# Eight PSUM tiles of one bank each in place of one tile of four banks and four of one

## The chip, the cores and the metric

The kernel runs on one core of a Trainium2 chip. The metric is the device time of one execution in microseconds (us), the median of three. The core has five engines with a queue each: TensorE (PE: matmuls and transposes, results in PSUM), VectorE (DVE), ScalarE (ACT), GpSimd (POOL) and SyncE (SP, which issues the DMAs here). PSUM has eight banks of 512 fp32 columns per partition. Instructions of one queue run in order.

## The reference

Two blocks. The first is a linear attention whose features are products of two sketches; the second takes its output as tokens and runs causal softmax attention in four experts, of which each token uses the best two.

```python
def phi(x):                                   # q, k: (4, 4, 1088, 32), 8 x 8 = 64 features
    a = np.einsum('rd,bhsd->bhsr', S1, x)
    b = np.einsum('rd,bhsd->bhsr', S2, x)
    return np.einsum('bhsi,bhsj->bhsij', a, b).reshape(*x.shape[:-1], r * r)
q_p, k_p = phi(q), phi(k)
kv = np.einsum('bhsf,bhsd->bhfd', k_p, v)
z = np.sum(k_p, axis=2)
x = einsum(q_p, kv) / (einsum(q_p, z) + 1e-6)   # then (4, 1088, 128)

logits = x @ w_gate                           # 4 experts, the best 2 of each token
w = softmax of the two chosen logits
for e in range(4):
    a = softmax(causal((x @ wq[e]) @ (x @ wk[e]).T / 8))
    out += (weight of e, 0 if not chosen) * (a @ (x @ wv[e]) @ wo[e])
```

## The kernel before

The kernel computes each token for its two chosen experts only. `wq` and `wk` of an expert are multiplied into one matrix `Mq[e]`, `wv` and `wo` into `Mo[e]`, so keys and values are `x` itself. A "slot" is one of the two chosen experts of a token. 64 tokens with two slots make a tile of 128 rows; a batch has 17 such tiles in three groups of 6, 6 and 5 (`groups`).

A batch goes through these steps, each a function that records jobs:

- `prepare`: DMAs bring k, q, v. VectorE transposes k and q (L404 to L414). PE multiplies them with the sketch matrices (`sketch`, L434), ScalarE copies the sketches out (L444), VectorE or GpSimd multiplies them into features (L454). PE sums features times v (`sums`, L489), ScalarE copies the sum out (`kvz`, L496). PE transposes q's features (L503), ScalarE copies (L507). PE forms numerators and denominators (`numer`, L524), VectorE divides (`divide`, L532 to L535), PE transposes the result x (L541), ScalarE copies it (L545), and SP stores x and reads it back in another layout (`xr`, L550, L557). Then PE computes the logits (L585), VectorE transposes them (L590) and ranks the experts (`choose`, L608 to L615), GpSimd makes the weights (`parts_of`, L653 to L664). The masks of the chosen experts go through DRAM (L618, L623, L627); for the first group of the first batch PE widens them with a one-hot matrix instead (L636, copies L641).
- `weights`, once: PE transposes the weights (L316), ScalarE copies them (L328, L330), PE multiplies them (L321), ScalarE copies (L335).
- `queries` of a group: PE projects x with each `Mq[e]` (L707), ScalarE copies two of the four (L726), VectorE picks by mask (L717).
- `scores` of a tile: PE (L749), then VectorE takes them out of PSUM with the causal mask and the maximum (L754), ScalarE exponentiates (L769, L771), VectorE takes the reciprocal (L774), GpSimd scales (L778), VectorE transposes in blocks (L783).
- `values` of a group: PE multiplies the weights with `xr` (L805) in four row groups of the array, each into a PSUM bank of its own (index `g`). The four sums lie in `V`. ScalarE copies them for the outer experts (`keep`, L829) and widens their masks (L832), GpSimd multiplies both (`outer`, L836). For the inner experts VectorE multiplies V with the mask (`inner`, L839) and patches it with the other half of V (`patch`, L843).
- `outputs` of a group: PE projects with `Mo[e]` (L863), ScalarE copies (L871), SP stores (L877).

PSUM is laid out by hand: tile `V` takes four banks, four more tiles `bank0` to `bank3` take one each, and pools hand them out:

```python
V = pp.tile([128, 4, 512], F32, tag="V", name="V")
banks = [pp.tile([128, 512], F32, tag=f"bank{x}", name=f"bank{x}") for x in range(4)]
ps=banks,
ps0=[V[:, x] for x in range(3)],
V=[V[:, :, 0:192]],
```

`ps0` serves the first batch's preparation and the weights, before the first values need V. The fourth bank of V takes matmuls on a constant (`nothing`, L927), which keep PE busy where it has no work yet.

The order of all jobs is the string `ORDER`, worked out beforehand by a planner: two letters name a job, `--` is one idle matmul. Each engine's queue is this order, cut down to its own jobs. Waits between engines are not in the string: the framework sets them from the tiles that each instruction reads and writes.

Of the kernel before, what the change touches and what calls it, by code (L numbers as in the profile page):

```python
# [9 lines left out]
F32 = mybir.dt.float32  # L10
# [56 lines left out]


ORDER = """
AAACAEASADATAUABAQARAPAVAWANAFAOAKAMALAZAHAJAGAIAb------------------------------------------------------------------  # L70
------------------AdAeAf--AhAgAaAiAjAc------AlAYFlAXAkAnAm--ApFmAoAvArAqAtAyA0AsAzAwA1AuB6FpAxA4FnB7A2FoA5B8FqA3A6Fr
B9A7----BFFsFuFwBGF2FxFyFzF4--BOBJF3F1BHBPBIF5----BZFtBSBQF0BaBRF9FvA8F6F+F/GDA9F7BbGEGFBcA+BAF8BvB+A/GAGKGGB/CABKBw
CGBMB1CEBxGBCHB2CIBWCFB3BUCBBTBLGLCDBNCCBzBXGMBVCJBCBYGCBdBEByBBGJBDGIB4------------BeBmBoBfBpBn--BiBqBgBjB5BkBrGHBh
BlCKBsC2C7CL------------GPCMGRGQB0CNGVGSGTGWCmGUCaCnCsCbCoBtCOCtDHBuCcCpCPDJCqCQCdDMCeCrDICRDKCfCgCSDOEJEEChDLCuDQCU
CTEZDNCiCvEVDPCwCjDlCVEWCkCxCWDnDmKoClD1KqDoCXKpDdDpD2CYKnD3DeDqCZEXDrD4CyEcD5KsDsKmCzEYD6D7EbDvEdKrC0D8DXC4C1C6C9C3
DRC5DtDYC8DSEaDZDuDfEeDTGNDaDgDbDwGODUDhC+GXDVDcC/DxDWGYDADyDBDiGbKwDzKvEfDjDCFYDDEvD0FTDEDFEhDkDGEnKtEgD9EoEiGgEwEj
KuGpGhD+EkGqGkElGiGZGjGrGtEmGaG0GsGyG1G2GzHHG3G4FDHILED/LGLFLHFBE/G5EALJG8FAFCG6LKEBFELIG+FFK+HAECLAFGK/FHK3G9ELEIED
EGExG7K5EKEMK4HFFIHBG/EFE3HGEyHCE4EpEzEHE5EqE0EPErE6EOE1HDE7EsHLHKHMEtE2KxPnK6ENKyEuKzHEJWH8K9HOJYPoH3K8E8JXHJEQJdJZ
JaE9HNETIIJcERJeESHnK7IJE+EUHbHtK0HoFJLBHcHpHuFKK1HdHqHvHeHrHhPwIMHfK2IKHsHgFLHiILLDIPHjIOLLGeHkLCIQGdPuGcLMGfHlHwPx
HxLQPtLNHmLOPqHyLRFMPrPvLPPpFNPsHVLYHWHXHPLZFOHYFPHQGlHZHRGoHaGnFQHSHTGmLcHUFRLaGuFVFSLSGxFXFaFUINLbGvFWLTGwLzFbFZIR  # L80
LhL0HzLiImLlLjInIoLkI2IpISIqI3IuITL1IrIUIvIsFdL2IVItI4IWFeIXI5IgFgI6IYIeIZH0I7IaIfI8IhJbIiIbIwJfIcLUI9LWLVH1IdLXLqIj
IxH2IkH+H7KAIyLrH4FcH9KBLuLsH/JFKCLtIlJiFfJKKDFkL3FhH5JgFiL4FjH6KEJhIBKFJjKGICIzL5I0JqJkIAKHJoJlL6I1IDKUIGPyJmKZJpIH
I+IEPzJrKIL7P0JnJsL/J4P1KJL9JwMBP2IFMCJtMIJ5J6JxMDMJL8JyJ7MAMKJ8JzL+MGNLJ0J9JuMEI/MFNMJvJ+MHJAMNP3MMNJJ/NNNKMOJBJ1J2
NPJCNQNRJDJ3QFJJJMJEJLOcJHQHOXJNQGJGJIMLOYNOQIMPKKNSQKNfNhQJNgKLNiQLNjMQMoMRNkMSJQNlMpMTMqMUJONmMrMiMsJPMjMkMWKMOLMX
MlOGMmJRKNLfMYJSJUMZKOMaJVLeLdKPJTLgKQLnLmLoOZLpKROeOaOdKSOgP/LyMVKTMbLvKYMnMuKVQALxMtQBMcLwKbKaNnMvN3MdQCMwNoN5KcMe
QDMxN4P4MfN6ObMyP5KWNpN7MgKXMzQEKfMhP6NqKeP7N8NrOfQPN9KhNsQRQQQVP8N+QSKdQWP+QTM9NtOxKgM4KiP9M0QUNuKkKjOyKlQNQMNvQOQi
NwQZQjM1QaQmM2QdQbM/M3NTM8M6M5QcQXNANZQYM7M+NUQrNaNVNCQsNbNDNWQvNcNXQtNBNdNYQuNeQ4NENxPVQ5NFPaOpNINyNHNzPBNGOqQ0PCOr
Q1N0QkN1OsPFQlPDOtN2Q2PEN/OuPGOvQ3PHQ6OAOBOwQ7OCRCQ+PIPJRDRAODREQ8PKOEO7OFOIOKONO5Q/OJOOOzRBOHO6RHQ9O0OMOhRFRIO8O1RJ
RGOiOQO9O2O3OPRORKORO+O4O/OjOSRNSEOURMPASJOVSVOTOWRLOkSWRQOlSXRPSZScR3SYOmOnSbR1SdRlR2RROoRnRmPLR4RoR5RtRSRvRuRpPMR6
RwR7RTRqPNRrR8RxPOQgRURsRVQhQfRyRdRWRzQeRXReR0PPRYPQRZPRQqRaRbQnQoPSRcQpPTRfQyPcPUTnQwPZPXPWQzPdSaQxToPYPbTlRgSeRhTp  # L90
TrS3TtTmRiTsS5RjS4TBRkS/S6TDTAS7SpTCTESnS8TFS9SxSoR9SqS+SrPeTGSsTHSvR+StTISuR/SwSASySzSBSCS0S1SfSGSDSISLPgSFSgPfS2SK
PiShSHUXSMUcTqPhSiSOPmTuSjPjPlUHPkSNSkUISlUJSPSmTvSQUNUKTYTwSRULT7TxSSUOTJSUTTUMUPSTTyT8TzT1TKT9UQT0T2URT3T+TLT/UST4
UAT5TMT6TNUBTOUCUDTPUEUFTQUGTRTaTXTSTVTZTbTWTUUTUUUVTdUeUWUbUZUYTcUfUaUdTeTfUgTgTkTjUhTiThUiUjUkUnUmUl
"""


# [1 line left out]
def kernel(  # L98
# [35 lines left out]
    def several(name, n, shape, dt=F32):  # L134
        return [const(f"{name}{x}", shape, dt) for x in range(n)]

    V = pp.tile([128, 4, 512], F32, tag="V", name="V")
    banks = [pp.tile([128, 512], F32, tag=f"bank{x}", name=f"bank{x}") for x in range(4)]

    atw = max(2 * t1 * (t1 - t0) * 32 for t0, t1 in groups)  # L140
    pools = dict(
        ps=banks,
        ps0=[V[:, x] for x in range(3)],
        V=[V[:, :, 0:192]],
        kin=several("kin", 1, [128, S]),
        qin=several("qin", 1, [128, S]),
        vp=several("vp", 1, [128, NJ, H, D + 1]),
# [194 lines left out]
    def prepare(b, rank):  # L342
# [114 lines left out]
        for s, nm in enumerate(("k", "q")):  # L457
            for x, (j0, j1) in enumerate(cuts):
                at = rank(0.05 + 0.12 * s + 0.06 * x)
                nj = j1 - j0  # L460
                ts = [(ps, nm, b, x, m) for m in range(2)]
                job("PE", 0.153 * nj * (1.6 if early else 1), at, lambda nm=nm, x=x, ts=ts: sketch(nm, x, ts),
                    [(nm + "T", b, x), "SKW"], ("sk", nm, b, x), [(nm + "T", b), ts[0], ts[1]])
                for m in range(2):
                    job("ACT", (0.027 * nj + 0.05) * (3 - parts), at, lambda nm=nm, x=x, m=m, ts=ts: sketch_copy(nm, x, m, ts),
                        [("sk", nm, b, x)], ("abc", nm, b, x), [ts[m], ab[nm]])
                need = [("abc", nm, b, x)]
                if not early:
                    job("POOL", 0.17 * nj + 0.12, at, lambda nm=nm, j0=j0, j1=j1: sketch_add(nm, j0, j1),
                        need, ("ab", nm, b, x), [ab[nm]])  # L470
                    need = [("ab", nm, b, x)]
                pool = not early or (nm == "q" and x == 1)
                step = 2 if pool else nj
                for y0 in range(j0, j1, step):
                    y1 = min(y0 + step, j1)
                    eng, us = (nc.gpsimd, 0.48) if pool else (nc.vector, 0.27)
                    job("POOL" if pool else "DVE", us * (y1 - y0) + 0.08, at,
                        lambda eng=eng, nm=nm, y0=y0, y1=y1: features(eng, nm, y0, y1),
                        need, ("fp", nm, b, x), [ab[nm], fps[nm]])
# [28 lines left out]

        for n, y0 in enumerate(range(0, 2 * NJ, 4)):
            y1 = min(y0 + 4, 2 * NJ)  # L510
            t, at = (ps, "tq", b, n), rank(0.3 + 0.05 * n)
            job("PE", 0.109 * (y1 - y0), at, lambda y0=y0, y1=y1, t=t: turn_features(y0, y1, t),
                [("fp", "q", b, 0)] + ([("fp", "q", b, 1)] if y1 > 8 else []), ("tq", b, n), [fps["q"], qpT, t])
            job("ACT", 0.107 * (y1 - y0) + 0.05, at, lambda y0=y0, y1=y1, t=t: keep_features("ACT", y0, y1, t),
                [("tq", b, n)], ("qpT", b, n), [t, qpT])
# [44 lines left out]
        for n in range(3):  # L560
# [5 lines left out]
                [("kvz", b)] + [("qpT", b, y) for y in range(last + 1)], ("num", b, n), [qpT, kvz, ts[0], ts[1], xs])  # L566
            job("DVE", 1.1, at, lambda x0=x0, x1=x1, ts=ts: divide(x0, x1, ts),
                [("num", b, n)], ("xs", b, n), [ts[0], ts[1], xs])
            t = (ps, "tx", b, n)
            job("PE", 0.33, at + 0.1, lambda x0=x0, x1=x1, t=t: turn_x(x0, x1, t),  # L570
                [("xs", b, n)], ("tx", b, n), [xs, t, xT])
            job("ACT", 0.37, at + 0.1, lambda x0=x0, x1=x1, t=t: keep_x(x0, x1, t), [("tx", b, n)], ("xT", b, n), [t, xT])
# [220 lines left out]
    def values(b, n, rank):  # L793
# [5 lines left out]
        def block(j0, j1):  # L799
            a = plan[AT][:, 0 : J * nt * 32].rearrange("p (j t s) -> p j (t s)", t=nt, s=32)  # L800
            for j in range(j0, j1):
                lo = 32 * max(0, j // 2 - t0)
                for g in range(4):
                    rows = slice(32 * g, 32 * g + 32)
                    nc.tensor.matmul(plan[Vk][:, g, lo : 32 * nt], plan[(f"xr{j // 12}", b)][rows, j % 12], a[rows, j, lo:],  # L805
                                     start=(j == 0), stop=(j == J - 1))

        def cost(j0, j1):
# [10 lines left out]

        uw = ("uw", b, n)  # L820

        def halves(a):
            return a.rearrange("p (h s) -> p h s", h=2)

        def part(x):
            return plan[Vk][:, 2 * x : 2 * x + 2, 0 : 32 * nt]

        def keep(x):
            nc.scalar.copy(halves(plan[uw][:, x, 0:w]), part(x))  # L829

        def widen(x):
            nc.scalar.copy(plan[agg][:, 3 * x, 0:w], plan[mb][:, 3 * x, 0:w])  # L832
# [3 lines left out]
            nc.gpsimd.tensor_tensor(out=a, in0=a, in1=plan[uw][:, x, 0:w], op=ALU.mult)  # L836

        def inner(x):
            nc.vector.tensor_tensor(out=halves(plan[agg][:, 1 + x, 0:w]), in0=part(x),  # L839
                                    in1=halves(plan[mb][:, 1 + x, 0:w]), op=ALU.mult)  # L840

        def patch(x):
            nc.vector.copy_predicated(halves(plan[agg][:, 1 + x, 0:w]), halves(plan[mb][:, E + x, 0:w]), part(1 - x))  # L843

        r = rank + 0.1
        for x in range(2):
            job("ACT", w * 0.00084 + 0.05, r, lambda x=x: keep(x), [("V", b, n)], ("uw", b, n, x), [Vk, uw])
            job("ACT", w * 0.00094 + 0.05, r - 0.05, lambda x=x: widen(x), [("mb", b, n)], ("agw", b, n, x), [agg, mb])
            job("POOL", w * 0.0023 + 0.08, r, lambda x=x: outer(x), [("uw", b, n, x), ("agw", b, n, x)], ("agg", b, n), [uw, agg, mb])
            job("DVE", w * 0.00104 + 0.08, r, lambda x=x: inner(x), [("V", b, n)], ("agg0", b, n, x), [Vk, agg, mb])  # L850
            job("DVE", w * 0.00104 + 0.08, r, lambda x=x: patch(x), [("agg0", b, n, x)], ("agg", b, n), [Vk, agg, mb])

    def outputs(b, n, rank):
        t0, t1 = groups[n]
# [69 lines left out]
        if b + 1 < B:  # L924
            prepare(b + 1, lambda x, b=b: 100.0 * b - 15 + 90 * x)
    def nothing():
        nc.tensor.matmul(V[:, 3], idle[:, 0:128], idle, start=True, stop=True)  # L927

    with tc.manual_schedule():
        plan.run(places(ORDER), nothing)  # L930
# [30 lines left out]
```

## Time and profile before

| | |
|---|---|
| median of three runs | 346.62 us (343.88 to 348.26) |
| profiled execution | 346.73 us, its span 345.0 us |
| PE busy | 313.2 us, 91% of the span |
| VectorE, ScalarE, GpSimd busy | 206.5, 138.9, 142.4 us |
| granted clock of PE, mean | 0.935 |
| values, L805: PE | 86.3 us |
| idle matmuls, L927: PE | 20.9 us, 65 of them |

The span runs from the first to the last instruction of one profiled execution. A timeline row reads: start, duration (us), engine, line, operation, output <- input, engine rows of the array where it is a matmul, shape, count, and in brackets the idle time of the engine before it with what ended it. A stage row of the table by stretches reads: stretch, length, then busy time and instruction count of PE, of its weight loads, of VectorE, ScalarE, GpSimd, then the granted clock, the share of DMA time and GB/s. An fp32 matmul shows as two records, so counts of rows are twice those of the code.

### The profile page before, as it was taken

Reading aid. Unit: us, or ns where it says so; the run is one execution under the profiler, and the core shown is the slowest. Engines: PE = TensorE matmul, PEld = TensorE weight load, DVE = VectorE, ACT = ScalarE, POOL = GpSimd, SP = SyncE. Lnnn points to the kernel's source line nnn. Section 1 sums busy time; section 2 is a strip of 40 time slices with the busy share of each in tenths; the row PEclk is TensorE's granted clock in tenths of the full one; section 3 lists DMA queues with packets and bytes.
Section 4 is the critical chain, followed back from the end, with each engine's and each line's share of the span. In section 5 each row is a group of like instructions: output and inputs, shape, how many; then the busy total and the mean of one; then the engine's idle time right before and its main releaser. Section 6 shows DMA issues by size and latency. Waiting matters only on the chain.

```text
span 345.0 us, 11306 instructions
## 1 busy us (share of the span) xinstructions
PE 313.2 (91%) x4739; PEld 228.1 (66%) x4739; DVE 206.5 (60%) x626; ACT 138.9 (40%) x401; POOL 142.4 (41%) x235
## 2 busy tenths in 40 slices
PE   8875879689989989999999999999999999999792
PEld 3563647356657656796775779787685585788692
DVE  4440241425989668746799853755788867866320
ACT  1113223118462266433556435462635443446110
POOL 5130445512332379711337663572257142434220
PEclk9995566959999999999999999999999999999987
DMA  7745017990001165199011201941103048001001
GB/s 170 152 69 65 27 46 167 190 162 0 2 2 48 44 153 80 43 163 191 2 40 41 83 2 39 190 77 54 42 6 97 25 93 169 0 6 42 3 2 42
DMA packets 79039, 24.39 MB, mean 71 GB/s; under 512 B 51084, under 2 KB 77964, under 8 KB 78988
## 3 DMA queue, kind: packets, MB, share of 16 engines
q1 hardware_dynamic: 78972, 23.66, 33.5%
q8 instruction: 37, 0.61, 0.8%
q14 instruction: 14, 0.11, 0.1%
q10 hardware_dynamic: 16, 0.00, 0.0%
HBM read 19.18 MB, written 4.48 MB: 69 GB/s over the span
## 4 chain that ended last, share of the span: by engine, by line
PE 77%; DVE 14%; ACT 5%; issue 2%; POOL 0%; DVEq 0%; ACTq 0%
PE V L805 22%; PE bank L749 16%; PE bank L863 8%; PE bank L707 8%; PE V L927 6%; DVE A L754 3%; DVE agg L839 2%; PE bank L489 2%; PE V L636 2%; ACT uw L829 2%; PE bank L434 2%; DVE AT L783 2%; PE bank L524 2%; PE bank L503 2%; DVE agg L843 2%
## 5 line engine op out<-in xcount | busy, mean ns | idle before, releaser
L778 POOL TENSOR_SCALAR A<-A,rs,sh 128x320 f32<-128x320 f32 (+15 forms) x68 | 55.8, 823 | 95.5 <-DVE rs L774 88.1
L749 PE MATMUL bank<-xT,qs 128*128 128x384 f32 (+11 forms) x216 | 79.6, 486 | 1.8 <-DVE mx L754 1.3
L769 ACT ACTIVATE A<-A,mx 128x320 f32<-128x320 f32 (+15 forms) x68 | 52.5, 772 | 58.6 <-DVE mx L754 55.4
L783 DVE STREAM_TRANSPOSE AT<-A 128x320 f32<-128x320 f32 (+15 forms) x68 | 50.9, 763 | 9.6 <-POOL A L778 9.1
L749 PEld LDWEIGHTS bank<-xT,qs 128*128 128x128 f32 x216 | 36.2, 189 | 24.7 <-issue 9.0
L805 PE MATMUL V<-AT,xra 32*128 32x192 f32 (+5 forms) x1152 | 48.8, 314 | 3.3 <-DVE agg L843 2.7
L805 PEld LDWEIGHTS V<-AT,xra 32*128 32x128 f32 x1152 | 43.0, 191 | 12.2 <-issue 5.8
L754 DVE CUSTOM_DVE_ANT_0 A<-bank,mask 128x384 f32<-128x384 f32 (+11 forms) x68 | 33.8, 507 | 22.9 <-PE bank L749 22.0
L707 PE MATMUL bank<-xT,Mq 128*128 128x384 f32 (+1 forms) x96 | 37.2, 503 | 2.4 <-DVE mx L754 1.5
L863 PEld LDWEIGHTS bank<-Mo,agg 128*128 128x128 f32 (+1 forms) x288 | 34.1, 185 | 6.6 <-issue 2.9
L863 PE MATMUL bank<-Mo,agg 128*128 128x128 f32 (+1 forms) x288 | 37.2, 280 | 0.6 <-DVE mx L754 0.6
L836 POOL TENSOR_TENSOR agg<-agg,uw 128x384 f32<-128x384 f32 (+1 forms) x24 | 22.5, 954 | 32.6 <-ACT uw L829 32.3
L717 DVE COPY_PREDICATED qs<-mb,bank 128x384 f32<-128x384 uint8 (+1 forms) x48 | 25.2, 553 | 10.3 <-PE bank L707 4.3
L927 PE MATMUL V<-idle 128*128 128x512 bf16 x65 | 20.9, 473 | 8.1 <-ACT mb L641 2.6
L805 PEld LDWEIGHTS V<-AT,xrb 32*128 32x128 f32 x768 | 25.9, 185 | 2.5 <-issue 2.3
L805 PE MATMUL V<-AT,xrb 32*128 32x160 f32 (+5 forms) x768 | 27.5, 290 | 0.0
L707 PEld LDWEIGHTS bank<-xT,Mq 128*128 128x128 f32 x96 | 17.2, 198 | 15.6 <-DVE mx L754 3.9
L754 DVE CUSTOM_DVE_ANT_0 A<-bank,mask,mx 128x320 f32<-128x320 f32 (+7 forms) x40 | 24.2, 612 | 2.5 <-PE bank L749 1.6
L839 DVE TENSOR_TENSOR agg<-V,mb 128x384 f32<-128x384 f32 (+1 forms) x24 | 12.8, 531 | 18.6 <-ACT uw L829 9.6
L829 ACT COPY uw<-V 128x384 f32<-128x384 f32 (+1 forms) x24 | 10.2, 463 | 32.5 <-DVE agg L839 26.3
L454 POOL TENSOR_TENSOR fp<-qab 128x512 f32<-128x512 f32 (+1 forms) x18 | 17.1, 968 | 11.1 <-ACT qab L444 11.0
L774 DVE RECIPROCAL rs<-rs 128x1 f32<-128x1 f32 x68 | 10.1, 151 | 13.8 <-ACT rs L771 13.7
(133 smaller groups left out, 372.3 us busy)
## 6 DMA issues: line engine op xcount, KB each, us to landing
xrb<-xd SPq DMA_DIRECT2D x16, 192.0 KB
xra<-xd SPq DMA_DIRECT2D x16, 192.0 KB
xrc<-xd SPq DMA_DIRECT2D x16, 160.0 KB
qin<-in_q_dram SPq DMA_DIRECT2D x16, 136.0 KB
mb<-md SPq DMA_DIRECT2D x7, 288.0 KB
kin<-in_k_dram SPq DMA_DIRECT2D x12, 136.0 KB
vp<-in_v_dram SPq DMA_DIRECT2D x12, 128.0 KB
xd<-xs SPq DMA_DIRECT2D x8, 192.0 KB
```

Of the source, the lines that this page charges most:

```text
L707: nc.tensor.matmul(plan[t][:, 0:w].rearrange("p (h t s) -> p h t s", h=2, s=32), Mq[:, e], xv, start=True, stop=True)
L717: nc.vector.copy_predicated(mine(l), halves(plan[mb][:, c, 0:w]), halves(plan[t][:, 0:w]))
L749: nc.tensor.matmul(plan[p][:, 0 : c1 - c0], plan[qs][:, 128 * t : 128 * t + 128], plan[xT][:, c0:c1], start=True, stop=True)
L754: nc.vector.tensor_tensor_reduce(out=plan[A][:, c0:c1], in0=plan[p][:, 0:w], in1=msk, scale=-1.0, scalar=mx[:, b, i, x - 1 : x] if x else ...
L769: nc.scalar.activation(out=a, in_=a, func=ACTF.Exp, bias=mx[:, b, i, last : last + 1], scale=-1.0, accum_out=zs[:, b, i : i + 1])
L778: nc.gpsimd.tensor_scalar(out=a, in0=a, scalar1=rs[:, b, i : i + 1], scalar2=plan[("sh", b)][:, i : i + 1], op0=ALU.mult, op1=ALU.mult)
L783: nc.vector.transpose(dst[:, 0 : keys // 32, t], plan[A][:, 0:keys].rearrange("p (j s) -> p j s", s=32))
L805: nc.tensor.matmul(plan[Vk][:, g, lo : 32 * nt], plan[(f"xr{j // 12}", b)][rows, j % 12], a[rows, j, lo:], start=(j == 0), stop=(j == J - 1))
L836: nc.gpsimd.tensor_tensor(out=a, in0=a, in1=plan[uw][:, x, 0:w], op=ALU.mult)
L839: nc.vector.tensor_tensor(out=halves(plan[agg][:, 1 + x, 0:w]), in0=part(x), in1=halves(plan[mb][:, 1 + x, 0:w]), op=ALU.mult)
L863: nc.tensor.matmul(plan[p][0:m, 128 * x : 128 * x + 128], plan[agg][:, e, 128 * x : 128 * x + m], Mo[:, e], start=(e == 0), stop=(e == E - 1))
L927: nc.tensor.matmul(V[:, 3], idle[:, 0:128], idle, start=True, stop=True)
```

## The change

- `V` is gone. There are eight tiles of one bank. `ps` holds `bank0` to `bank3` as before, `ps0` holds `bank4` to `bank6`, the values' four sums take `bank4` to `bank7` as a list of tiles, and idle matmuls write `bank7`.
- In the first batch only k's sketches, the sums, numerators, logits and masks still use `ps0`; q's sketches and both transposes (of features and of x) use `ps`.
- ScalarE copies all four sums into `uw`, bank by bank: four copies of half the width for two.
- VectorE's product and patch read `uw` in SBUF and no longer PSUM.
- The order of jobs is a new one, on all queues; it has 73 idle matmuls (65 before).

Line numbers behind the order move: L927 becomes L922, L829 L823, L832 L826, L836 L830, L839 L833, L843 L837, L863 L858, L877 L872.

```diff
-    V = pp.tile([128, 4, 512], F32, tag="V", name="V")
-    banks = [... for x in range(4)]
+    banks = [... for x in range(8)]
-        ps=banks,
-        ps0=[V[:, x] for x in range(3)],
-        V=[V[:, :, 0:192]],
+        ps=banks[0:4],
+        ps0=banks[4:7],
+        V=[banks[4:8]],
...
-                ts = [(ps, nm, b, x, m) for m in range(2)]
+                ts = [("ps0" if early and nm == "k" else "ps", nm, b, x, m) for m in range(2)]
...
-            t, at = (ps, "tq", b, n), rank(0.3 + 0.05 * n)
+            t, at = ("ps", "tq", b, n), rank(0.3 + 0.05 * n)
...
-            t = (ps, "tx", b, n)
+            t = ("ps", "tx", b, n)
...
-                    nc.tensor.matmul(plan[Vk][:, g, lo : 32 * nt], ...
+                    nc.tensor.matmul(plan[Vk][g][:, lo : 32 * nt], ...
...
-        def keep(x):
-            nc.scalar.copy(halves(plan[uw][:, x, 0:w]), part(x))
+        def keep(x, h):
+            nc.scalar.copy(plan[uw][:, x, 32 * nt * h : 32 * nt * h + 32 * nt], plan[Vk][2 * x + h][:, 0 : 32 * nt])
...
         def inner(x):
-            nc.vector.tensor_tensor(out=halves(plan[agg][:, 1 + x, 0:w]), in0=part(x),
-                                    in1=halves(plan[mb][:, 1 + x, 0:w]), op=ALU.mult)
+            nc.vector.tensor_tensor(out=plan[agg][:, 1 + x, 0:w], in0=plan[uw][:, x, 0:w],
+                                    in1=plan[mb][:, 1 + x, 0:w], op=ALU.mult)
         def patch(x):
-            nc.vector.copy_predicated(halves(plan[agg][:, 1 + x, 0:w]), halves(plan[mb][:, E + x, 0:w]), part(1 - x))
+            nc.vector.copy_predicated(plan[agg][:, 1 + x, 0:w], plan[mb][:, E + x, 0:w], plan[uw][:, 1 - x, 0:w])
...
-        nc.tensor.matmul(V[:, 3], idle[:, 0:128], idle, start=True, stop=True)
+        nc.tensor.matmul(banks[7], idle[:, 0:128], idle, start=True, stop=True)
```

## The prediction

> **What bounds the kernel now.** First the page's table of 40 slices: TensorE (PE) is busy 0.9 and more from slice 10 on, and ragged before; there the granted clock sags too. So I asked for stages, cut where the work changes:
>
> ```profile
> core 0: us, PE busy (x) PEld busy (x) DVE busy (x) ACT busy (x) POOL busy (x), PEclk, DMA share, GB/s
> 13.10:91.07 77.97, 62.26 (x899) 42.24 (x899) 29.31 (x95) 24.83 (x80) 25.11 (x53) 0.76 0.49 87
> 91.07:345.00 253.93, 239.01 (x3800) 181.17 (x3799) 171.68 (x505) 112.63 (x319) 110.87 (x159) 0.99 0.28 60
> ```
>
> 91.07 is where the first values matmul (L805) starts. From there PE is busy 239 of 254 us at clock 0.99: nothing on another engine counts much. Before it no engine is full, and PE, though 62 of 78 us "busy", runs at 0.76. What holds it, the timeline of PE shows with the releaser in brackets:
>
> ```profile
> 23.19 1.09 PE L503 MATMUL V<-ident,fp 128*128 128x128 f32 x8 [0.59 <-ACT qab L444]
> 24.96 1.24 PE L489 MATMUL V<-vp,fp 128*64 128x33 f32 x36 [0.68 <-ACT fp L507]
> 26.89 0.77 PE L316 MATMUL V<-ident,AT 128*128 128x128 f32 x4 [0.69 <-ACT fp L507]
> 28.05 1.08 PE L503 MATMUL V<-ident,fp 128*128 128x128 f32 x4 [0.40 <-ACT kvz L496]
> 29.90 1.09 PE L503 MATMUL V<-ident,fp 128*128 128x128 f32 x4 [0.77 <-ACT AT L328]
> ```
>
> L316 turns weights; it reads nothing that L507 (a copy of query features) makes. Both only touch V. So a write to one bank of V waits for the reader of another bank, and PE and ScalarE take turns. The turns delay all that follows: VectorE sits idle from 22.2 to 37.1, the gate's masks end at 74.96, the first scores come at 79.75.
>
> At the other end, the timelines of VectorE and PE around the last hand-over of V:
>
> ```profile
> 325.23 0.49 DVE L839 TENSOR_TENSOR agg<-V,mb 128x320 f32<-128x320 f32 x1 [0.89 <-PE V L805]
> 326.54 0.49 DVE L839 TENSOR_TENSOR agg<-V,mb 128x320 f32<-128x320 f32 x1 [0.82 <-ACT uw L829]
> 326.95 0.90 DVE L843 COPY_PREDICATED agg<-mb,V 128x320 f32<-128x320 uint8 x2
> 327.90 4.71 PE L805 MATMUL V<-AT,xra 32*128 32x192 f32 x96 [2.74 <-DVE agg L843]
> ```
>
> VectorE reads V, then ScalarE, then VectorE again: V is held 2.7 us after its last matmul. Elsewhere PE has other work during that.
>
> **The change, part by part.**
>
> *PE's work.* The new order issues the same matmuls. I priced each kind by its rate where the clock is 1.0 (a values matmul of 192 columns 0.094 us, a sketch 0.037, a query projection 0.65, an idle one 0.285). Ahead of the first L805 stand 38.5 us of real work before and 39.1 after; so what follows it is equal, and the gain or loss of the start goes through to the end. Idle matmuls: 42 at the very start in both, then 23 before and 31 after (8.8 us). Of the 78 us from 13.1 to 91.07, 38.5 + 6.6 is work at full clock, 15.7 is PE idle (77.97 - 62.26), and 17.2 is lost to the low clock.
>
> *The start.* With no waits it would take 39.1 + 8.8 = 47.9 us: first L805 at 61.0. I followed the new order through all queues with durations of the rows. Sketches of k from 13.1 end at 16.1; nine idle matmuls; the 72 of L489 end at 21.2 (their products, two copies and two VectorE products of 1.22 and 1.45 us, are ready at 18.2). Weights, q's sketches, eight L503 and the weight products follow without a wait to 27.6, as each goes to a bank of its own; their copies run beside them. First L524 ends 29.1, its division (1.15) 30.2, first L541 31.5 (before: 41.75). VectorE has transposes of q until 31.6, the second division until 33.5, the logits' transpose, then the choice of experts, 2.8 us by 61.52 to 64.3 before: masks' first matmul at 37.0 (before 64.39), PE waiting some 0.7. Six masks, copied by ScalarE and VectorE in turn (0.48, 0.56), end at 43.1. Last L541 44.4, logits 45.5, second choice 48.1 (2.2), last pick of group 0's queries 48.9: first score at 48.9 (before 79.75).
>
> From there VectorE sets the pace. Until group 0's last L783 its queue holds eleven L754 (5.7 us by their widths), eight L717 (4.3), seven L783 (3.0) and nine short ones (1.4): 14.4 us, and 2.2 of waits for GpSimd (L778): 65.5, and PE idles beside it. The first of group 1's picks (L717) comes at 56; its masks, fetched from DRAM, must be there. Narrowed (L618) at 48.9 and stored and fetched at the 5.7 us that L618 to fetch took before (53.3 to 59.0), plus 0.54 MB at the 190 GB/s of slice 7, 2.8 us: 57.4, about in time. My walk leaves out hops between engines, and the clock may dip. I allow 3.5 us: **first values at 69, bounds 61 and 75; -22 us (-30 to -16).**
>
> SP's queue: two loads of v go ahead of k's, so k comes about 1 us later; its transposes end at 10.9 instead of 9.9, under the 42 idle matmuls (else 1 us). The third xr group now follows the mask fetch; it is first read some 25 us of PE work after the first L805.
>
> *ScalarE.* 24 copies (480 and 429 ns) become 48 of 192 and 160 columns. Rows of 160 columns take 295 ns and of 256, 372; I take 320 and 295: 15.0 instead of 10.2 us, +4.8, hidden in ScalarE's 141 idle us after 91. V is free after four copies, 1.3 us, bank 0 after one. At 325 that removes 2.4 us of the 2.7; elsewhere V's release ended no wait above 0.6.
>
> *VectorE.* Its 48 products and patches now read two SBUF tensors instead of one and V. Without company the price is the same (L454, two SBUF inputs, 1.22 us for 1024 columns, is 0.5 for 384; before 0.55). With company it is not:
>
> ```profile
> 51.09 0.68 DVE L608 TENSOR_TENSOR beats<-L 128x33 f32<-128x33 f32 x6
> 61.52 1.70 DVE L608 TENSOR_TENSOR beats<-L 128x18 f32<-128x18 f32 x6
> 60.17 2.68 POOL L454 TENSOR_TENSOR fp<-qab 128x512 f32<-128x512 f32 x3
> ```
>
> The first stands where GpSimd is idle, the second, smaller, under L454: 1.0 us more, about one GpSimd instruction. Both L608 inputs are in SBUF. In each of 12 groups four such operations (2.2 us) now meet two GpSimd products (1.9): 0 to 1.9 us a group, 0 to 23 in all, and up to 46 if each of the 48 waits 0.95 for some GpSimd instruction. VectorE has 82 idle us after 91 to take it, but what it does late, PE waits for next: scores' banks (L754) and projections. Nearest is the L608 row, one wait in six instructions: 48/6 x 1.0 = 8 us on VectorE. It is 68% busy, so I put a little under half on PE: **+3.5 (0 to 23).**
>
> The Trainium skill says it as a rule (SBUF — State Buffer, "Who interferes with whom"): a VectorE instruction with two SBUF inputs contends with a GpSimd instruction that reads SBUF, while one with a single SBUF input does not. That speaks against this change, and the L608 rows agree. By the rule each of the 48 would pay whenever it meets a GpSimd instruction, half of a 0.95 us one on average and 44% of the time: 10 us on VectorE as an estimate, 4.4 instead of 3.5 in the sum.
>
> *The tail.* After the last values ScalarE copies four banks (1.3) before VectorE's second product can start; before, the first product started at once. GpSimd's 1.96 and VectorE's 2.2 may alternate: ready at 4.5 to 4.8 us after the last matmul instead of 3.2 (332.54 to 335.75). PE has the other group's 24 projections, 2.9 us, meanwhile: +1 (0 to 2).
>
> **Sum.** 345.0 - 22 - 2.4 + 3.5 + 1 = 325.1 us of span; the profiled execution took 346.73, 1.73 more than its span: 326.8. That execution is at the median, 346.62. I say 326.
>
> **Rivals.**
> (1) *A transfer takes the place of the false waits.* Group 1's masks hold VectorE. For: DMA is over 0.9 busy from 51 to 77.6 in the old run, so the masks may have landed only 24 us after L618; their first use at 85.4 shows no wait. Then 48.9 + 24 = 73 for the picks, and VectorE's 9.5 us from there (56 to 65.5): first values at 82.5, -8.6; time 340, no change. Against: the fetch now stands ahead of the next batch's loads.
> (2) *The port eats half.* Contention puts 12 us instead of 3.5 on PE: 335. For: the L608 row. Against: VectorE's idle time.
> (3) *Slower.* Each of the 48 operations waits 0.95 us for GpSimd, and all of it reaches PE, because VectorE is late with L754: +45.6, minus 23.4: 369. It decides from (23.4 + 6.9) / 48 = 0.63 us on PE for each of the 48. Against: GpSimd is busy 44%, VectorE 68%.
> (4) *It doesn't do what it says.* The waits are of the data, not of the tile: 346. Against: L316.
>
> **How the numbers follow.** Forecast 0.72 (own range 314 to 334), (1) 0.10, (2) 0.10, (3) 0.04, (4) 0.04. The range 314 to 340 reaches from a start without waits, 345 - 30 - 2.4 + 1.7, to rival 1. About 2% is what a measurement of this kernel tells from no change: the forecast and (2) are faster, with a third of (1); (3) is slower; the rest the same: 0.85, 0.11, 0.04.
>
> **What would show it.** Right: no ScalarE releaser in front of L316 and L503 in the start; clock near 0.95 from 13 to 69; first L749 near 49, first L805 near 69; after it as long as before, 254 us within 5; no 2.7 us gap ahead of the last L805 group. Contention shows as L833 and L837 above 0.7 us in the mean. Wrong: a DMA ahead of L717 near 56; the first L805 after 80; or PE idle above 25 us after it.

## The result, and the profile after

The changed kernel took 330.85 us (median of 4 executions, 329.60 to 335.74) where the kernel before, measured beside it, took 347.44: a ratio of 0.954, 95% interval 0.943 to 0.966 (here and below a ratio is taken over the executions that a lower clock didn't disturb, a median over all). The forecast was 326, with a range of 314 to 340. The execution that was profiled took 329.67 us, with a span of 327.9.

Cut at the first values matmul (L805) as before, the windows of the changed kernel read (stage, length, busy time of PE, PEld, DVE, ACT, POOL, then the granted clock):

```profile
13.10:69.25 56.15, 52.48 (x952) 35.70 (x950) 32.39 (x101) 25.86 (x82) 22.65 (x50) 0.97 0.62 111
69.25:327.90 258.65, 243.12 (x3762) 182.10 (x3755) 181.78 (x499) 113.64 (x341) 120.32 (x161) 0.99 0.28 61
```

The opening is 21.8 us shorter, at a clock of 0.97 in place of 0.76. What follows it is 4.7 us longer. The timeline of PE in the opening, where ScalarE's readers stood in brackets before:

```profile
20.46 0.66 PE L316 MATMUL bank<-ident,AT 128*128 128x128 f32 x4
...
24.55 1.09 PE L503 MATMUL bank<-ident,fp 128*128 128x128 f32 x8
...
27.57 1.31 PE L503 MATMUL bank<-ident,fp 128*128 128x128 f32 x10
...
37.62 1.39 PE L636 MATMUL bank<-cT,AT 64*128 64x192 f32 x4 [2.24 <-DVE den L532]
```

L316 and L503 of the first batch wait for nobody now. One gap above 0.7 us is left, 2.24 us ahead of the first mask matmul (L636), while VectorE chooses the experts:

```profile
33.18 2.48 DVE L608 TENSOR_TENSOR beats<-L 128x18 f32<-128x18 f32 x6 [0.53 <-POOL fp L454]
```

The six instructions of this shape took 1.70 us before, partly under GpSimd's L454, and 2.48 here, under more of it. The larger six (128x33) took 0.68 us beside an idle GpSimd, in both kernels.

The last hand-over of the banks, in the timeline of PE:

```profile
311.62 3.36 PE L805 MATMUL bank<-AT,xra 32*128 32x192 f32 x96 [0.77 <-ACT uw L823]
314.91 3.49 PE L858 MATMUL bank<-Mo,agg 128*128 128x128 f32 x26
318.62 2.97 PE L858 MATMUL bank<-Mo,agg 128*128 128x128 f32 x22 [0.22 <-DVE agg L837]
```

The wait fell from 2.74 to 0.77 us, and the block behind it from 4.71 to 3.36: before, it had run in a window at 0.66 of the clock.

```profile
327.90:332.60 4.70, 4.70 (x97) 4.66 (x97) 0.00 (x0) 0.00 (x0) 0.04 (x1) 0.66 0.02 3
```

(That is the kernel before, in the windows view.) Last, the groups by form (count, busy time, mean ns of one), the kernel before first, then the changed one:

```profile
L836 POOL TENSOR_TENSOR agg<-agg,uw 128x384 f32<-128x384 f32 x16 | 15.7, 999 | 20.1 <-ACT uw L829 19.9
L843 DVE COPY_PREDICATED agg<-mb,V 128x384 f32<-128x384 uint8 x16 | 8.7, 575 | 0.0
L839 DVE TENSOR_TENSOR agg<-V,mb 128x384 f32<-128x384 f32 x16 | 8.9, 554 | 13.8 <-ACT uw L829 7.2 <-PE V L805 6.6
```

```profile
L830 POOL TENSOR_TENSOR agg<-agg,uw 128x384 f32<-128x384 f32 x16 | 19.6, 1242 | 21.9 <-ACT uw L823 21.9
L837 DVE COPY_PREDICATED agg<-mb,uw 128x384 f32<-128x384 uint8 x16 | 14.1, 889 | 0.2 <-ACT uw L823 0.2
L833 DVE TENSOR_TENSOR agg<-uw,mb 128x384 f32<-128x384 f32 x16 | 13.8, 880 | 4.0 <-ACT uw L823 4.0
```

Over both widths VectorE's products and patches cost 14.0 us more and GpSimd's products 4.6. The 48 copies of ScalarE have a mean of 324 ns; their busy time is 11.5 us against 10.2.

### The profile page after: what moved, and what is told of

Same layout as the page of the kernel before. It is cut to its first block, busy times and chain, and to the rows that moved or that the text cites. A ratio compares the mean times of both kernels' runs of the same rounds, so it can differ in the third digit from the quotient of the medians.

```text
span 327.9 us, 11366 instructions
## 1 busy us (share of the span) xinstructions
PE 307.5 (94%) x4747; PEld 222.6 (68%) x4747; DVE 220.9 (67%) x626; ACT 141.0 (43%) x425; POOL 149.4 (46%) x235
## 4 chain that ended last, share of the span: by engine, by line
PE 72%; DVE 17%; ACT 4%; issue 3%; POOL 1%; ACTq 0%; DVEq 0%
PE bank L805 22%; PE bank L749 13%; PE bank L858 10%; PE bank L707 7%; PE bank L922 6%; PE bank L434 3%; DVE A L754 3%; DVE agg L837 3%; PE bank L489 3%; PE bank L503 3%; DVE agg L833 3%; PE bank L524 2%; DVE AT L783 2%; DVE qs L717 2%; ACT A L769 2%
## 5 line engine op out<-in xcount | busy, mean ns | idle before, releaser
L778 POOL TENSOR_SCALAR A<-A,rs,sh 128x256 f32<-128x256 f32 (+16 forms) x68 | 56.6, 835 | 78.6 <-DVE rs L774 73.3
L749 PE MATMUL bank<-xT,qs 128*128 128x320 f32 (+11 forms) x216 | 80.1, 489 | 3.1 <-DVE mx L754 1.9
L769 ACT ACTIVATE A<-A,mx 128x512 f32<-128x512 f32 (+15 forms) x68 | 52.5, 773 | 54.4 <-DVE mx L754 50.2
L783 DVE STREAM_TRANSPOSE AT<-A 128x256 f32<-128x256 f32 (+15 forms) x68 | 51.4, 765 | 10.4 <-POOL A L778 10.1
L749 PEld LDWEIGHTS bank<-xT,qs 128*128 128x128 f32 x216 | 36.6, 189 | 29.1 <-issue 7.9
L805 PE MATMUL bank<-AT,xra 32*128 32x192 f32 (+5 forms) x1152 | 46.5, 305 | 2.6 <-issue 1.8
L805 PEld LDWEIGHTS bank<-AT,xra 32*128 32x128 f32 x1152 | 41.6, 185 | 10.6 <-issue 5.1
L830 POOL TENSOR_TENSOR agg<-agg,uw 128x384 f32<-128x384 f32 (+1 forms) x24 | 27.1, 1147 | 35.8 <-ACT uw L823 35.8
L754 DVE CUSTOM_DVE_ANT_0 A<-bank,mask 128x448 f32<-128x448 f32 (+11 forms) x68 | 33.7, 508 | 10.8 <-PE bank L749 10.3
L707 PE MATMUL bank<-xT,Mq 128*128 128x384 f32 (+1 forms) x96 | 38.1, 503 | 2.7 <-DVE qs L717 1.2
L858 PE MATMUL bank<-Mo,agg 128*128 128x128 f32 (+1 forms) x288 | 39.0, 287 | 1.4 <-DVE rs L774 0.6
L858 PEld LDWEIGHTS bank<-Mo,agg 128*128 128x128 f32 (+1 forms) x288 | 35.1, 191 | 6.9 <-issue 4.9
L805 PE MATMUL bank<-AT,xrb 32*128 32x160 f32 (+5 forms) x768 | 28.0, 292 | 0.0
L805 PEld LDWEIGHTS bank<-AT,xrb 32*128 32x128 f32 x768 | 25.8, 185 | 2.6 <-issue 2.1
L833 DVE TENSOR_TENSOR agg<-uw,mb 128x384 f32<-128x384 f32 (+1 forms) x24 | 19.6, 830 | 11.0 <-ACT uw L823 11.0
L707 PEld LDWEIGHTS bank<-xT,Mq 128*128 128x128 f32 x96 | 16.4, 194 | 13.7 <-DVE mx L754 2.9
L454 POOL TENSOR_TENSOR fp<-qab 128x512 f32<-128x512 f32 (+1 forms) x18 | 17.2, 971 | 14.7 <-ACT qab L444 14.5
L922 PE MATMUL bank<-idle 128*128 128x512 bf16 x73 | 20.5, 428 | 1.2 <-DVE A L210 1.2
L837 DVE COPY_PREDICATED agg<-mb,uw 128x384 f32<-128x384 uint8 (+1 forms) x24 | 19.6, 824 | 0.2 <-ACT uw L823 0.2
L726 ACT COPY qs<-bank 128x384 f32<-128x384 f32 (+1 forms) x24 | 10.9, 459 | 20.5 <-PE bank L707 15.8
```

The source lines that it names most:

```text
L707: nc.tensor.matmul(plan[t][:, 0:w].rearrange("p (h t s) -> p h t s", h=2, s=32), Mq[:, e], xv, start=True, stop=True)
L749: nc.tensor.matmul(plan[p][:, 0 : c1 - c0], plan[qs][:, 128 * t : 128 * t + 128], plan[xT][:, c0:c1], start=True, stop=True)
L754: nc.vector.tensor_tensor_reduce(out=plan[A][:, c0:c1], in0=plan[p][:, 0:w], in1=msk, scale=-1.0, scalar=mx[:, b, i, x - 1 : x] if x else ...
L769: nc.scalar.activation(out=a, in_=a, func=ACTF.Exp, bias=mx[:, b, i, last : last + 1], scale=-1.0, accum_out=zs[:, b, i : i + 1])
L778: nc.gpsimd.tensor_scalar(out=a, in0=a, scalar1=rs[:, b, i : i + 1], scalar2=plan[("sh", b)][:, i : i + 1], op0=ALU.mult, op1=ALU.mult)
L783: nc.vector.transpose(dst[:, 0 : keys // 32, t], plan[A][:, 0:keys].rearrange("p (j s) -> p j s", s=32))
```

## The experiments

The questions: is the tile what shortened the opening, or the order; what is contention worth on TensorE; and where do the 4.7 us go. All medians and traces together (idle is PE's, from 13.1 us to the first values; the clock is that of this stage; "rest" is from the first values to the end of the span):

| kernel | first values | idle | clock | rest | median us | ratio to before, 95% |
|---|---|---|---|---|---|---|
| before | 91.07 | 15.7 | 0.76 | 253.93 | 347.4, 345.8, 344.4, 345.1 | |
| changed | 69.25 | 3.7 | 0.97 | 258.65 | 330.85 | 0.954 (0.943-0.966) |
| e0, changed, again | 66.56 | 4.3 | 1.00 | 258.74 | 333.3 | 0.966 (0.938-0.994) |
| e1, one tile | 76.41 | 8.4 | 0.89 | 256.99 | 336.0 | 0.976 (0.970-0.983) |
| e2, old order, split | 68.55 | 6.8 | 0.94 | 249.85 | 321.5 | 0.942 (0.936-0.948) |
| e3, PSUM products | 74.46 | 4.6 | 0.86 | 252.54 | 328.1 | 0.962 (0.956-0.969) |
| e4, small outer | 75.46 | 4.6 | 0.86 | 252.64 | 329.6 | |
| e5, late fetch | 66.00 | 4.2 | 1.00 | 254.40 | 322.9 | 0.938 (0.929-0.947) |
| e6, gap filled | 66.14 | 2.4 | 1.00 | 254.46 | 322.8 | 0.939 (0.932-0.946) |
| e6 again | 67.33 | 2.6 | 1.00 | 254.57 | 323.7 | 0.938 (0.934-0.941) |
| e7, e2 + gap filled | 66.06 | 5.3 | 1.00 | 249.64 | 321.1 | 0.935 (0.926-0.945) |
| e8, e3 + e6 | 65.95 | 2.4 | 1.00 | 248.45 | 316.8 | 0.918 (0.915-0.922) |
| e9, e7 + hand-over | 70.40 | 6.5 | 0.97 | 248.00 | 318.6 | 0.923 (0.918-0.928) |

The four medians of the kernel before belong to four measurements: the changed kernel's, that of e0 to e3, that of e4 to e7, and that of e6 again with e8 and e9; each ratio is to the kernel before in the same measurement. What is said below rests on the stages of the traces first, and on the totals beside them.

**e0: the changed kernel again.** No edit.

> The changed kernel once more, as it is, for a second trace. In the first trace TensorE stood for 1.81 us from 212.0 to 213.82 in the middle of a block of the values' sums, with no releaser the profile could name, just after 6 us in which the DMA engines were busy without a break with the tiles xrb and xrc; the clock then fell to 0.85, 0.50 and 0.79 in three stretches of 2 us, which is 1.7 us more. Theory: this gap belongs to the order of the transfers, and it comes again at the same place, with 330 to 331 us in all. Rival: it is a chance event of one execution; then the new trace has no such gap and a span about 3 us shorter (325 us), and the contention on VectorE explains hardly anything of the time after the first values.

The gap came again, after the same 14 of 32 matmuls: 1.86 us. It is no chance. The timeline of PE in the first trace and the windows after it:

```profile
211.08 0.93 PE L805 MATMUL bank<-AT,xra 32*128 32x192 f32 x14
213.82 1.02 PE L805 MATMUL bank<-AT,xra 32*128 32x192 f32 x18 [1.81 <-issue]
```

```profile
214.00:216.00 2.00, 2.00 (x68) 1.76 (x68) 0.19 (x2) 0.00 (x0) 0.00 (x0) 0.85 0.37 107
216.00:218.00 2.00, 2.00 (x11) 2.00 (x11) 0.90 (x4) 0.48 (x1) 0.00 (x0) 0.50 0.05 14
218.00:220.00 2.00, 2.00 (x21) 1.77 (x20) 0.00 (x0) 0.44 (x2) 0.00 (x0) 0.79 0.24 68
```

"Issue" says that no engine's semaphore was late. The second cost is in the clock column behind it: 0.15 + 0.50 + 0.21 of 2 us each, 1.7 us. The total I expected was missed, because the opening differed: 2.7 us shorter at a clock of 1.00, and the other three executions took 331.5 to 335.2.

**e1: one tile, new order.**

```diff
-    banks = [pp.tile([128, 512], F32, tag=f"bank{x}", name=f"bank{x}") for x in range(8)]
+    V = pp.tile([128, 4, 512], F32, tag="V", name="V")
+    banks = [pp.tile([128, 512], F32, tag=f"bank{x}", name=f"bank{x}") for x in range(4)]
+    banks += [V[:, x] for x in range(4)]
```

> The new order, the copies bank by bank and the products from SBUF are kept; only the four value banks are again slices of one tile. Theory: the waits of the opening on banks that nobody shares come back, the clock falls with them, and the first block of the values' sums starts near 80 us (bounds 75 and 91) in place of 69; at the hand-overs of the banks TensorE waits for all four copies in place of the first, about 1 us more; in all 341 to 346 us. Rival, that the new order alone made the gain: first values at 69 to 71 us, 330 to 333 us in all.

First values at 76.41, inside the bounds of the theory, but the total, 336.0, lies between the two. The false waits are back, now even in front of the idle matmuls that should hold the clock (timeline of PE, e1, where the idle matmul is L924):

```profile
45.56 0.58 PE L924 MATMUL V<-idle 128*128 128x512 bf16 x1 [1.67 <-ACT mb L643]
...
50.65 2.29 PE L924 MATMUL V<-idle 128*128 128x512 bf16 x5 [1.23 <-ACT mb L643]
```

An idle matmul reads nothing that L643, a copy of masks, touches; it only shares the tile. But the new order alone, with its use of other banks for q's sketches, features and the transposes of x, had already cut the opening from 78.0 to 63.3 us: 14.7 of the 21.8 us, more than the 11 that the theory left to it (80 in place of 91). At the last hand-over TensorE waited 1.00 us in place of 0.77, not the 1 us more that I expected.

**e2: the split alone, old order.** The products stay on PSUM, one instruction for each bank.

```diff
-    V = pp.tile([128, 4, 512], F32, tag="V", name="V")
-    banks = [... for x in range(4)]
+    banks = [... for x in range(8)]
...
-        ps=banks, ps0=[V[:, x] for x in range(3)], V=[V[:, :, 0:192]],
+        ps=banks[0:4], ps0=banks[4:7], V=[banks[4:8]],
...
-            nc.scalar.copy(halves(plan[uw][:, x, 0:w]), part(x))
+            for h in range(2):
+                nc.scalar.copy(halves(plan[uw][:, x, 0:w])[:, h], part(x, h))
```

> The old order and the products from PSUM, with the four banks as tiles of their own; the copy and each product become two instructions, one for each bank. Theory: the split alone takes away most of the waits of the opening: first values at 72 to 77 us in place of 91.07, so a gain of 14 to 19 us; the hand-over to the last block near the end stays (2.7 us), VectorE and GpSimd don't get in each other's way; in all 328 to 334 us. Rival, that the gain needs the new order: first values after 85 us, and 340 us or more in all.

It did more than the theory asked: first values at 68.55, 321.5 us. The windows of e2, cut as before:

```profile
13.10:68.55 55.45, 48.70 (x827) 34.77 (x833) 30.37 (x95) 24.39 (x80) 25.18 (x53) 0.94 0.71 122
68.55:318.40 249.85, 237.74 (x3800) 180.33 (x3799) 174.06 (x553) 114.59 (x343) 111.08 (x159) 0.99 0.27 61
```

So each of the two, split and order, takes away most of the false waits; they overlap. And the changed kernel, which has both, is slower than the split alone, by 9.3 us in its first median and by 11.8 in e0, measured beside e2. In the traces 8.8 us of that lie after the first values (258.65 against 249.85). The rest of the runs look for these 9 us.

**e3: products from PSUM again, new order.** In the four groups left out, the next group's sums are ordered ahead of the last products.

```diff
+        psum = (b, n) not in ((1, 1), (1, 2), (3, 1), (3, 2))
...
-            nc.vector.tensor_tensor(out=plan[agg][:, 1 + x, 0:w], in0=plan[uw][:, x, 0:w], ...)
+            for c, v in sources(x):   # two banks of V if psum, else uw
+                nc.vector.tensor_tensor(out=plan[agg][:, 1 + x, c], in0=v, ...)
```

> The changed kernel with its order untouched, but in 8 of the 12 groups of tokens VectorE's products read the values' sums from the PSUM banks, two instructions of half the width each, as the old kernel read them; the other four groups stay as they are, since in them the next group's sums are ordered ahead of the last products. Theory, that VectorE and GpSimd hold each other up when both read SBUF: in the 8 groups the products take 0.5 to 0.6 us for a full width in place of 0.83, GpSimd's come down from 1147 to about 1000 ns, VectorE has 8 to 9 us less to do, and 1.5 to 3.5 us of that comes off the time: 327 to 329 us. Rival, that the longer products lie beside TensorE's work: VectorE's work falls the same, the time stays within 1 us of the changed kernel's in this call. A second rival, that two short instructions cost as much as one slow one: no fall in VectorE's work.

The rest fell by 6.1 us, more than expected, and the median by 2.7 to 5.2 only (against the two medians of the changed kernel), since this trace's opening took 7.9 us longer than e0's with the same instructions up to there. VectorE gave back 7.2 us (181.73 to 174.49), a little under the 8 to 9 expected: two half products take some 690 ns together and not 500 to 600. The difference of the openings first. Timeline of PE, e0, then e3:

```profile
36.56 0.92 PE L636 MATMUL bank<-cT,AT 64*128 64x192 f32 x4 [2.23 <-DVE den L532]
37.40 1.56 PE L707 MATMUL bank<-xT,Mq 128*128 128x384 f32 x4
38.89 2.21 PE L636 MATMUL bank<-cT,AT 64*128 64x192 f32 x12
```

```profile
36.61 1.64 PE L636 MATMUL bank<-cT,AT 64*128 64x192 f32 x4 [2.35 <-DVE den L532]
38.18 2.93 PE L707 MATMUL bank<-xT,Mq 128*128 128x384 f32 x4
41.04 4.21 PE L636 MATMUL bank<-cT,AT 64*128 64x192 f32 x12
```

The same gap in both; behind it the same matmuls at full clock in one and half clock in the other. In the windows of e3 the granted clock is 0.50 from 36 to 53 us; in e0 it is 1.00, in the first trace of the changed kernel 0.50 for 3 us. The Trainium skill (TensorE: Matmul & The Clock Gate, "What's actually happening") has the clock fall after an idle window of some 3.4 us that runs free of the kernel, so that an event depends on where in the window it falls. The difference between equal executions agrees with that; the length doesn't: here 2.35 us and, in the middle, 1.81 us of idle were enough.

**e4: GpSimd nearly out of it.** The kernel leaves out all but 2 columns of GpSimd's products, so its outputs for two of the four experts are not the reference's.

```diff
-            nc.gpsimd.tensor_tensor(out=a, in0=a, in1=plan[uw][:, x, 0:w], op=ALU.mult)
+            nc.gpsimd.tensor_tensor(out=a[:, 0:2], in0=a[:, 0:2], in1=plan[uw][:, x, 0:2], op=ALU.mult)
```

> The changed kernel, but GpSimd's outer products work on the first 2 of their 384 or 320 columns, so that nearly all of GpSimd's work beside VectorE's products is left out; order, copies and sources stay. Theory, that the two engines hold each other up: VectorE's full-width products fall from 0.83 us to the 0.45 to 0.6 us of its shortest ones, 24 x 2 of them by some 13 us in all, though they still read both operands from SBUF; with GpSimd's wait gone too, 3 to 7 us less from the first values to the end (258.7 us). Rival, that two operands from SBUF are slow in themselves: VectorE's products stay at 0.75 us or more, and the time from the first values to the end falls by less than 2 us.

Groups by form of e4:

```profile
L833 DVE TENSOR_TENSOR agg<-uw,mb 128x384 f32<-128x384 f32 x16 | 11.2, 713 | 5.3 <-ACT uw L823 5.3
L837 DVE COPY_PREDICATED agg<-mb,uw 128x384 f32<-128x384 uint8 x16 | 9.2, 582 | 0.2 <-ACT uw L823 0.2
```

The patches fall from 889 to 582 ns with the same sources in SBUF: it is the company, not the source. The products fall only to 713 (the median over both widths to 550), because some still meet other work of GpSimd: in e4's timeline one of 320 columns takes 1.42 us from 138.12, beside L454, and those with nothing beside them 0.47 to 0.49. So the 13 us I expected came to 10.1 (VectorE's busy time in the rest, 181.73 us in e0 and 171.64 here). The rest is 252.64, the same 6 us as e3. Here GpSimd's own products are shorter too, 287 ns in place of 1147, so this run doesn't say through which of the two engines TensorE gained.

**e5: the fetch of xrc later.** In the order of the transfers on SP's queue:

```diff
-xrc<-xd2 x4, xd3<-xs x4, out<-ob
+xd3<-xs x4, out<-ob, xrc<-xd2 x4
```

In `ORDER` the four stand 41 to 51 places later, not the 25 that the text below gives.

> The changed kernel; only the four transfers of the tile xrc for the third batch are issued some 25 jobs later, behind the stores of xs, so that they no longer come right after the four of xrb. The gap without a releaser was found in all four traces with the new order, at the same matmul (after 14 of 32 in the first block of the third batch's values), 1.65 to 1.93 us long. Theory: TensorE waits there for its next piece of program, which the transfers hold up; with the transfers apart the gap falls under 0.5 us, and with it the clock loss behind it, 2 to 3.5 us from the first values to the end (258.7 us). Rival: the matmuls before it are so short that the program can't be brought on fast enough, whatever the transfers do; then the gap stays at 1.6 us or more.

The gap is gone, the block is one row in the timeline of PE, and the clock stays at 1.00:

```profile
207.51 1.48 PE L805 MATMUL bank<-AT,xra 32*128 32x192 f32 x32
```

The rest fell from 258.74 to 254.40: 4.3 us, above the 2 to 3.5 expected.

**e6: the opening's gap filled.**

```diff
 # ORDER: ahead of the job ("mask", 0)
+----------------        (8 idle matmuls)
```

> The changed kernel with 8 more idle matmuls ahead of the first mask matmul of the opening, where TensorE stood 2.2 to 2.4 us waiting for VectorE in every trace of the new order. Theory: that gap is what brings the clock down in most executions (0.50 for 12 us behind it in one of them, not at all in another: 74.5 and 66.6 us to the first values with the same instructions), so that with the gap filled the clock stays at 1.00 there in every execution: first values at 66.5 to 68 us, median 327 to 329 us in place of 331 to 333, and executions that differ by under 4 us. Rival, that the clock falls by chance or by the work around it: still 331 to 335 us and a spread of 6 to 8 us. Beside it, a test of the gap in the middle: 16 more instructions are ahead of it in TensorE's program; if the gap stands where a piece of the program ends, it now comes 8 matmuls earlier, after 6 of the 32; if it belongs to that matmul, it stays after 14.

First values at 66.14; executions from 322.35 to 323.83, all at a clock of 0.996 or 0.997. The repetition below gave six more within 0.9 us. The changed kernel itself spread over 6 to 8 us. The clock bears the theory out: of the 20 executions with the gap unfilled (changed kernel, e0, e3, e4, e5) 13 had a mean clock of 0.971 or less, of the 16 with it filled (e6 twice, e8) none below 0.993. (In e3 the half clock lasted 17 us, not the 12 of the text above.) The median, 322.8, came under the 327 to 329 expected, because of the middle. In the middle I was wrong twice over: the gap neither moved nor stayed, it vanished (rest 254.46), with the transfers untouched. So it hangs on both: on what the transfers do and on which instructions stand where. The DMA view of one microsecond of e0, then of e6, shows the rows that could tie them (q8 carries program pieces of some 16 KB, 37 in a run; share of 16 engines last):

```profile
q1 hardware_dynamic: 349, 0.17, 114.1%
q8 instruction: 1, 0.02, 8.8%
```

```profile
q1 hardware_dynamic: 388, 0.19, 114.9%
q8 instruction: 1, 0.02, 8.5%
```

The first is 208 to 209 us in e0, just ahead of the gap (209.32 to 211.18), at the end of the 6 us of transfers. The second is 204 to 205 in e6; e0 has no such packet in that microsecond. So in e6, and at the same time in e5, the piece came 4 us sooner. That the wait is for this piece is argued, not shown. The Trainium skill (Runtime: NRT & Kernel Launch, "Instruction fetch mechanics") says that the program streams in by a queue of its own in 16 KiB blocks, mostly hidden; the size agrees with the packets here, and in the five traces with the gap it was not hidden, if it is this.

**e7: the same in the old order.** e2 with 8 idle matmuls ahead of ("mask", 0).

> The old order with the four banks as tiles of their own (the kernel that took 321.5 us), with 8 more idle matmuls ahead of the first mask matmul, where its trace has a gap of 2.0 us and behind it a clock of 0.87 and 0.57 in two stretches of 6 us, which is 3.4 us lost. Theory: the gap is filled, the clock stays at 1.00 there, first values at 65 to 66 us in place of 68.55, 316 to 318.5 us in all. Rival, that the clock doesn't hang on that gap: 320 to 322 us, first values at 68 to 69.

The profiled execution did as the theory said, 317.53 us and first values at 66.06, at a clock of 1.00. The other three had a mean clock of 0.978 to 0.984, and the median is 321.1: one gap was filled, and others (1.34 us ahead of a transpose of x, a gap of 1.02 by "issue") are left in this order. Not settled by this run alone.

**e6 again, e8: contention at an undisturbed clock.** e8 is e6 with e3's products.

> The changed kernel with the 8 idle matmuls of before, once more, as the measure for the next kernel: first values at 66 us, 254.5 us from there to the end, 322 to 324 us in all, every execution at a clock above 0.99. If the steadiness was chance, some executions fall to 0.97 and 330 us again.

> The same with the products read from PSUM in 8 of the 12 groups, so that the source of these products is all that differs from the kernel beside it, at the same undisturbed clock. Theory, that VectorE and GpSimd hold each other up and TensorE pays for it: 4 to 6 us less from the first values to the end (248.5 to 250.5 us in place of 254.5), 316.5 to 319 us in all. Rival, that the 6 us seen with the products from PSUM came from the slow opening of that execution, in which the other engines could work ahead: 253 us or more from the first values, 321 us or more in all.

Windows from the first values to the end, e6, then e8:

```profile
67.33:321.90 254.57, 240.83 (x3762) 180.27 (x3755) 181.66 (x499) 113.62 (x341) 119.95 (x161) 1.00 0.29 63
```

```profile
65.95:314.40 248.45, 238.16 (x3761) 180.43 (x3755) 174.38 (x531) 113.67 (x341) 115.25 (x161) 0.99 0.28 63
```

With equal openings the rest is 6.1 us shorter; the rival falls. VectorE gives back 7.3 us and GpSimd 4.7; the runs don't separate what each is worth to TensorE. Of the 6.1, 3.45 is idle time of PE (254.57 - 240.83 against 248.45 - 238.16); the other 2.7 lies within PE's busy rows. By form, 1.6 of it is in groups that also wait less: the projections (L858, in e8 L867, 33.8 to 33.0 us), L707 of 384 columns (19.3 to 19.0) and L749 of 352 (6.6 to 6.1). The remaining 1.1 isn't assigned. The groups by form of e8:

```profile
L830 POOL TENSOR_TENSOR agg<-agg,uw 128x384 f32<-128x384 f32 x16 | 16.3, 1039 | 18.8 <-ACT uw L823 18.7
L846 DVE COPY_PREDICATED agg<-mb,bank 128x192 f32<-128x192 uint8 x24 | 7.4, 363 | 0.0
L842 DVE TENSOR_TENSOR agg<-bank,mb 128x192 f32<-128x192 f32 x24 | 7.2, 347 | 3.8 <-ACT uw L823 2.2 <-PE bank L541 1.7
```

Two halves from PSUM, 694 ns, beat one whole from SBUF beside GpSimd, 876 in e6. At 316.8 us, 316.2 to 317.9, e8 beats the kernel before (ratio 0.918) and the changed one. Its rest, 248.45, is also below the 249.85 of the split alone: with contention (6.1) and the gap in the middle (4.3, e5) taken out, nothing is left of the 8.8 us that the changed kernel was slower there.

**e9: the old order with the other gaps and the hand-over.** e7 with 5 and 2 idle matmuls ahead of two transposes of x, in one group the changed kernel's way, and near the end of `ORDER` two jobs (`Ta` and `TS`) in each other's place:

```diff
+        src = uw if (b, n) == (3, 2) else Vk
```

> The old order with the split and its filled gap, to which are added 5 and 2 idle matmuls ahead of the two transposes of x that TensorE waits 1.34 and 0.58 us for, and, in the last but one group alone, the changed kernel's way of products from SBUF, so that ScalarE's copies release the banks for the last block. Theory: the hand-over falls from 2.0 to 0.8 us (1.2 us), the clock stays at 1.00 through the opening in more executions: 314.5 to 316.5 us in the best and a median of 315 to 318. Rival, that the gaps at the transposes don't matter and the last products, held up by GpSimd, are late for the projection: 317 us in the best and a median near 321 as before.

The hand-over did its part: PE waited 0.36 us in place of 2.01, and the rest is the shortest of all, 248.00. Three of six executions took 317.0, the other three 320.2 to 320.7. In the profiled one PE lost 1.6 and 1.4 us in the opening to two "issue" gaps, which the idle matmuls don't cover. The median of 318.6 is between the two theories.

## Why the prediction came out as it did

**The opening (-22 us; measured -21.8).** Right in cause: e2, with the split and nothing else, has it, and the bracketed readers are gone; e1 adds that the new order with its other banks has two thirds of it without the split. The walk through the queues held at full clock: first score at 48.9 by the walk, 48.92 in e0 (51.62 in the first trace); group 1's picks at 56 by the walk, 56.19 in e0 (58.89), without a wait for masks, which ends rival 1; first values at 65.5 before the 3.5 us allowed, 66.56 in e0. Two things were not right. That the size fits to 0.2 us is luck: with the same instructions the first values came at 66.6, 69.3 or 74.5, as the clock took the gap or not. And the 0.7 us I gave to PE's wait for the choice of experts was 2.24: the masks' first matmul came at 37.62 and not 37.0, since L608 took 2.48 us and L611 0.56, in my price 1.70 and 0.18, and PE was ready at 35.4 and not 36.3. This gap is the one that the clock falls behind.

**k's transposes (10.9; measured 11.0).** Right by luck. They start at 8.10 us as before (8.08), so k was not late; what made them late is that two small copies of VectorE between them took 1.45 us in place of 0.33, beside GpSimd's copy of v (rows at the end).

**The hand-over (-2.4).** 2.74 to 0.77, so -2.0, and another -1.35 from the block behind it, which had run at 0.66 of the clock. I had priced the wait and not the clock behind it.

**The copies (hidden).** Hidden; 324 ns in the mean, some 310 by the estimate. The busy time grew by 1.3 us and not 4.8: I had set a sum of durations (15.0) against a busy time (10.2), in which copies overlap.

**The port (+8 on VectorE, +3.5 on PE).** The term that failed, in size. On VectorE it was 14.0 us, 0.29 for each of the 48, where the L608 row had been read as one wait of 1.0 in six. And "a little under half" of it on PE was far too little: in e8, which frees 8 of 12 groups, PE got back 6.1 us for 7.3 on VectorE and 4.7 on GpSimd, an engine to which my term gave nothing. VectorE is idle more than a quarter of that time (181.66 of 254.57 us busy in e6), but the idle time doesn't absorb the loss. The rule cited in the prediction (the Trainium skill, SBUF — State Buffer, "Who interferes with whom") agrees with both engines here, GpSimd's products too (for an input count of one it holds only outside the 2-port modes, a condition that the prediction left out); the estimate of 10 and 4.4 us from it was nearer and still low. Rival 2, at 12 us, named the right loss at twice its size.

**The tail (+1).** From the end of the last L805 to the end of the span 12.9 us against 12.4: +0.5; in e8, without contention there, 12.15.

**What the sum lacked.** The gap in the middle and its clock, +4.3 (e5), and fewer short waits: the ten others that the timeline of the kernel before shows after the first values sum to 5.6 us, those of e8 to 2.9: -2.7. With these, 253.93 - 2.0 - 1.35 + 6.1 + 4.3 - 2.7 = 258.3, against 258.65 measured (the tail is within the 6.1; four groups of e8 still pay for contention, and no run shows what). So the forecast's span of 325.1 came within 3 us of 327.9 although single terms were off by up to 4.3, because their errors partly cancel; the median lies another 1.2 us above the profiled execution.

## What to carry to other kernels

Give each PSUM bank that has its own reader a tile of its own before anything else: the split alone took 24 us off, and with the change's order, copies and sources it was 16.6 and 12.5 in two measurements. Before an instruction's source moves from PSUM to SBUF to release a bank earlier, ask who else reads SBUF at that time, and take that way only where the release is waited for, as at one hand-over of twelve here. Then look through TensorE's timeline for single gaps of 2 us and fill them: their price is in the clock behind them, it differs from execution to execution, and a single trace may not show it. Filling one is not always enough: in the old order (e7), where gaps of 1.34 and 1.02 us stayed, the median did not move (321.1 against 321.5).

## What was not expected of the hardware

- A gap of 2.2 to 2.35 us on TensorE halved the granted clock for 3 to 17 us in some executions and not at all in others; 8 idle matmuls (2 us) in it took the first values to 66 to 67 us in each of three traces (e6 twice, e8).
- TensorE can stand 1.65 to 1.93 us for no semaphore, at the same instruction in five traces of four kernels that share an order; later transfers, or 16 instructions more ahead of it, both end it.
- Two small copies of VectorE (32 x 32, one SBUF source) took 1.45 us as GpSimd copied beside them, and 0.33 in the kernel before, where that copy starts only at 11.22; here the 42 idle matmuls cover it. The timeline of VectorE, then of GpSimd, in the changed kernel:

```profile
8.69 1.45 DVE L296 COPY SKW<-A 32x32 f32<-32x32 f32 x2
```

```profile
9.06 1.05 POOL L383 COPY vp<-A 128x1024 f32<-128x1024 f32 x1
```
